# Linear attention and a gated feed-forward layer on one core: queries loaded behind the turned keys, with a new issue order

## The chip, the core and the metric

The kernel runs on one core of a Trainium2 chip. A core has a matrix engine (TensorE, PE in the profile), a vector engine (VectorE, DVE), an activation engine (ScalarE, ACT), a general engine (GpSimd, POOL) and a synchronisation engine (SyncE, SP). Each runs its own instructions in order and waits on semaphores for the others. Transfers between the chip's memory (HBM), the on-chip memory (SBUF) and back run on 16 DMA engines; here GpSimd issues the loads that change float32 into bfloat16, and SP issues the transposes inside SBUF and the stores of the output. TensorE writes its results to eight banks of PSUM, which the other engines read.

The metric is the time of one execution on the device in microseconds (us), the median of several. A profiled execution shows when each instruction ran; its span runs from the program's first instruction to its last.

## What is computed

The inputs are float32: q, k and v of 8 batches, 8 heads, 1024 positions and 64 features; E and F of 64 x 1024; the weights of the layer, 512 x 1536 twice and 1536 x 512.

```python
k_proj = np.einsum('ks,bhsd->bhkd', E, k)
v_proj = np.einsum('ks,bhsd->bhkd', F, v)
scores = (1.0 / np.sqrt(64)) * np.matmul(q, k_proj.transpose(0, 1, 3, 2))
scores = scores - np.max(scores, axis=-1, keepdims=True)
attn = np.exp(scores)
attn = attn / (np.sum(attn, axis=-1, keepdims=True) + 1e-09)
attn_out = np.matmul(attn, v_proj)
x = attn_out.transpose(0, 2, 1, 3).reshape(8 * 1024, 512)
gate = 1.0 / (1.0 + np.exp(-(x @ w_gate)))
out = (gate * (x @ w_val)) @ w_out
```

The 1024 positions of k and v are projected to 64, so that a query meets 64 keys. The output has 8192 rows of 512.

## The kernel before

**Batches and blocks.** The attention goes batch by batch, counted from 0 here; the layer behind it goes in 16 blocks of 512 rows, two a batch. The first batch has code of its own (`first_batch`), with the first block of the layer in plain products. From then on the layer of one batch runs interleaved with the attention of the next, and with the loads of the one after.

**The attention of one batch.** Six loads bring its inputs, each 512 KB as stored in bfloat16: two halves (by heads) of K, of V and of Q (`load_kv`, `load_q`, both through `load`, line 557). K and V go to the two halves of one buffer, `KVs`. Q goes to `Qb`. Then:

- `transpose_q` (line 1438, on SP) turns the queries with four transposing transfers, `Qb` into `qT`.
- `kv` projects K and V, 16 matmuls on TensorE; ScalarE copies the results out, the keys into `kpd`, and `turn_kd` (line 1481, on SP) turns these with one transposing transfer into `kpD`.
- `score_pair` makes the scores of 128 queries in two banks; VectorE takes the maximum (`highest`, line 1590) and subtracts it (`lower`, line 1617); ScalarE writes the exponentials (`exps`) into the K half of `KVs`, which is called `pt` then.
- `turn_p` (line 1652, on SP) turns `pt` into `eT`, four transposing transfers a batch.
- `outs` multiplies with the projected values, VectorE inverts the sums, and VectorE or GpSimd divides (line 1699) into the V half of `KVs`, called `xt` then.
- `turn_x` (line 1716, on SP) turns `xt` into one of two buffers `xT`, four transposing transfers a batch.

So the K and V of the next batch can only be loaded when `pt` and `xt` have been turned. The queries have a buffer of their own, which is free as soon as `transpose_q` has read it.

**The layer.** The gate and value products of a block go in three quads (`quad_jobs`, `seven`): a 2 x 2 matrix of tiles is multiplied with seven products instead of eight, at the price of sums of tiles on VectorE and GpSimd (`xS`, `hT`, line 545, and lines 1102 and 1171) and copies on ScalarE (line 530). Its output product is made in the same way (`o_jobs`) for most blocks. Nearly all matmuls are of 128 x 128 weights and 256 columns, and all stand under line 516.

**The order.** The body is written as jobs, each for one engine. A table, `ORDER`, lists all jobs in the order in which they are issued, which fixes the order on each engine. A negative entry -m is a filler: a matmul of 256 m columns whose result nobody reads, during the start. A second table, `PLACES`, gives each result its PSUM bank or its SBUF buffer. Waits follow from the order: `add` records which tiles a job reads and writes, and each instruction waits for the last writers and readers of them that were issued before it. `ORDER` interleaves the engines, so one can count how many matmuls are issued between, say, a turn and the first matmul that reads it.

**The loads and what they wait for.** `loads` (line 1786) issues the six loads of a batch from 2 on. It is handed `after`, and each of the loads counts these as tiles that it reads:

```python
landed_x = lambda s: [("xTt", s, t, R) for t in range(4) for R in range(2)]
...
loads(2, AT["loads2"], landed_x(1))
...
loads(p + 2, base + AT["loads"], landed_x((p + 1) % 2))
```

So all six loads of a batch wait for the last `turn_x` of the batch in front. GpSimd issues them, and a load that waits holds up what stands behind it on GpSimd: divisions of the attention and sums of the layer. SP's queue is in order too: turns of queries, keys, probabilities and x, and the stores (line 1257).

Of the kernel before, what the change touches and what calls it, by code (L numbers as in the profile page):

```python
# [153 lines left out]
class Job:  # L154
# [189 lines left out]
class Scheduler:  # L344
# [4 lines left out]
    def job(self, eng, pos, body, release=0.0, name=""):  # L349
        self.jobs.append(Job(eng, body, name))  # L350
# [24 lines left out]
def bass_linformer_attn__then__ffn_glu_sigmoid_kernel(  # L375
# [20 lines left out]
    with contextlib.ExitStack() as es:  # L396
# [363 lines left out]
        job = sched.job  # L760
# [1118 lines left out]
```

## Time and profile before

| | us |
|---|---|
| median of three executions | 520.29 |
| lowest, highest | 520.05, 520.41 |
| the profiled execution | 520.55 |
| its span | 518.7 |
| VectorE busy | 434.2 (84%) |
| ScalarE busy | 373.0 (72%) |
| GpSimd busy | 171.5 (33%) |

TensorE's row and the waits are shown where the prediction uses them. TensorE had its full clock throughout. The profile gives DMA queues beside the engines: the loads from GpSimd are in the queue `software_dynamic`, the turns and stores from SP in `hardware_dynamic`. A DMA issue has two times: that of the issuing instruction, and that from its start to the landing of the data. In the order of time, a row holds the start, the time from the first to the end of the last instruction of the row, the engine, the line, the tiles (written, then read), the number of instructions, and in brackets the idle time of that engine in front, with what ended it.

### The profile page before, as it was taken

How to read it: one execution, taken by the hardware profiler on the slowest of the kernel's cores; microseconds unless marked ns; L12 is line 12 of the kernel's file. 1: busy time of each engine (PE TensorE's matmuls, PEld its weight loads, DVE VectorE, ACT ScalarE, POOL GpSimd, SP SyncE). 2: the span in 40 equal slices, each digit the busy share in tenths (PEclk: the TensorE clock that was granted, in tenths of full speed). 3: DMA queues.
4: the chain of work that ended last, by engine and by line, in shares of the span. 5: the costliest groups of instructions: out<-in, count | busy, mean ns of one | idle time of the engine just before them, and what ended most of it. 6: DMA issues, size and time to landing. Idle time of an engine off the chain costs nothing.

```text
span 518.7 us, 12593 instructions
## 1 busy us (share of the span) xinstructions
PE 510.6 (98%) x4954; PEld 418.9 (81%) x4954; DVE 434.2 (84%) x847; ACT 373.0 (72%) x714; POOL 171.5 (33%) x200
## 2 busy tenths in 40 slices
PE   8999999989999999999999999999999999999997
PEld 4557757878888888888888888888888878888884
DVE  6779998498988998889897899899977889958872
ACT  1558776877877787857977778876878669677752
POOL 9885005702226007340157003630243300450020
PEclk9999999999999999999999999999999999999999
DMA  9999949994579955995659935899448983352004
GB/s 165 197 198 207 174 78 174 146 192 124 99 144 168 178 132 95 191 182 137 103 104 206 191 113 90 159 204 158 86 102 165 191 155 83 62 121 84 1 2 162
DMA packets 140556, 71.61 MB, mean 138 GB/s; under 512 B 97232, under 2 KB 132304, under 8 KB 140496
## 3 DMA queue, kind: packets, MB, share of 16 engines
q1 hardware_dynamic: 104560, 40.91, 38.2%
q0 software_dynamic: 35936, 29.89, 37.2%
q8 instruction: 39, 0.64, 0.5%
q14 instruction: 21, 0.17, 0.1%
HBM read 60.29 MB, written 16.78 MB: 149 GB/s over the span
## 4 chain that ended last, share of the span: by engine, by line
PE 92%; DMA 4%; POOL 1%; DVE 1%; ACT 0%; issue 0%; POOLq 0%; ACTq 0%
PE pF L516 50%; PE pA L516 43%; DMA KVs<-in_k_dram 3%; DMA eT<-KVs 1%; POOL hT L545 1%; DVE topf L1590 1%; DMA kpD<-kpd 1%; DVE pF L1617 0%; ACT KVs L530 0%; POOL xS L545 0%; POOL KVs L557 0%; POOL Qb L557 0%; ACT EFT L530 0%; DVE pA L1617 0%; ACT ost L530 0%
## 5 line engine op out<-in xcount | busy, mean ns | idle before, releaser
L530 ACT ACTIVATE spare<-pF 128x512 f32<-128x512 f32 (+2 forms) x163 | 93.2, 580 | 40.0 <-PE pF L516 31.4
L530 ACT ACTIVATE spare<-pA 128x512 f32<-128x512 f32 (+2 forms) x157 | 87.0, 571 | 29.2 <-PE pA L516 18.7
L545 POOL TENSOR_TENSOR hT<-hT,hS 128x512 bf16<-128x512 bf16 x42 | 48.2, 1163 | 160.1 <-PE pF L516 84.2
L1699 POOL TENSOR_TENSOR KVs<-spare,inv 128x384 bf16<-128x384 f32 (+1 forms) x50 | 35.9, 730 | 106.2 <-PE pA L516 31.9
L516 PE MATMUL pF<-wO,hT 128*128 128x256 bf16 (+1 forms) x408 | 60.3, 291 | 0.0
L1171 DVE SCALAR_TENSOR_TENSOR hT<-spare,pA 128x512 bf16<-128x512 f32 x60 | 40.6, 680 | 14.2 <-PE pA L516 5.2
L1102 DVE TENSOR_TENSOR spare<-pA,spare 128x512 f32<-128x512 f32 x62 | 41.8, 682 | 12.1 <-PE pA L516 10.0
L530 ACT ACTIVATE spare<-spare 128x512 f32<-128x512 f32 x77 | 47.8, 628 | 4.8 <-DVE spare L1102 4.7
L516 PEld LDWEIGHTS pF<-wO,hT 128*128 128x128 bf16 x408 | 39.3, 98 | 11.8 <-issue 0.4
L1102 DVE TENSOR_TENSOR spare<-pF,spare 128x512 f32<-128x512 f32 x54 | 36.7, 684 | 10.7 <-PE pF L516 7.3
L1171 DVE SCALAR_TENSOR_TENSOR hT<-spare,pF 128x512 bf16<-128x512 f32 x57 | 38.6, 678 | 4.3 <-PE pF L516 2.7
L516 PE MATMUL pA<-xT,wV 128*128 128x256 bf16 (+1 forms) x208 | 34.4, 287 | 0.0
L516 PE MATMUL pA<-xT,wG 128*128 128x256 bf16 (+1 forms) x212 | 33.8, 283 | 0.0
L516 PE MATMUL pF<-xT,wG 128*128 128x256 bf16 (+1 forms) x196 | 32.6, 288 | 0.4 <-issue 0.4
L516 PE MATMUL pF<-xT,wV 128*128 128x256 bf16 (+1 forms) x200 | 32.4, 283 | 0.0
L516 PE MATMUL pF<-xS,tV 128*128 128x256 bf16 x216 | 32.3, 273 | 0.0
L516 PE MATMUL pA<-xS,tG 128*128 128x256 bf16 x208 | 31.1, 273 | 0.0
L516 PE MATMUL pA<-xS,wV 128*128 128x256 bf16 x200 | 29.7, 273 | 0.0
L516 PE MATMUL pF<-wT,hT 128*128 128x256 bf16 x216 | 28.3, 273 | 0.0
L516 PE MATMUL pA<-wO,hT 128*128 128x256 bf16 (+1 forms) x204 | 27.2, 279 | 0.0
L516 PE MATMUL pF<-wT,hS 128*128 128x256 bf16 x204 | 27.2, 273 | 0.0
L516 PE MATMUL pA<-xS,wG 128*128 128x256 bf16 x184 | 27.1, 272 | 0.0
(184 smaller groups left out, 1258.3 us busy)
## 6 DMA issues: line engine op xcount, KB each, us to landing
out_dram<-ost SPq DMA_DIRECT2D x63, 256.0 KB, 2.4
KVs<-in_v_dram POOLq DMA_DIRECT2D x15, 512.0 KB, 10.6
Qb<-in_q_dram POOLq DMA_DIRECT2D x14, 512.0 KB, 10.2
KVs<-in_k_dram POOLq DMA_DIRECT2D x14, 512.0 KB, 10.7
wO<-in_moe_w_out_dram POOLq DMA_DIRECT2D x1, 1536.0 KB, 12.8
KVs<-in_k_dram POOLq DMA_DIRECT2D x4, 256.0 KB, 6.5
Qb<-in_q_dram POOLq DMA_DIRECT2D x4, 256.0 KB, 9.1
wG<-in_moe_w_gate_dram POOLq DMA_DIRECT2D x4, 256.0 KB, 11.5
```

What stands on the lines that cost most here:

```text
L516: lambda e: e.matmul(o, lhsT, rhs, **kw),
L530: lambda e: e.activation(o, i, func, scale=scale),
L545: fn = lambda e: e.tensor_tensor(o, a, b, op)
L1102: lambda e: e.tensor_tensor(PB(b)[:, :] if stay else BF(s), PB(b)[:, :], BF(s), ALU.add),
L1171: lambda e: e.scalar_tensor_tensor(o, y.rearrange("p (j c) -> p j c", j=2), 1.0, x.rearrange("p (j c) -> p j c", j=2), ALU.add, ALU.mult,),
L1590: lambda e: e.tensor_reduce((top if by_pe(b, t, y) else topf)[:, n : n + 8], PB(bk)[:, :].rearrange("p (n k) -> p n k", n=8), mybir.AxisLi ...
L1699: fn = lambda e: e.tensor_tensor(xto.rearrange("p (g h d) -> p h g d", g=2, h=H)[:, hh[0] : hh[1], :, :], o[:, :, 0:DH].rearrange("p (h g) ...
```

## The change

Each load of queries of batches 2 to 7 now waits for the turned keys of the batch in front (`kpD`, written by `turn_kd`; for batch 2 by the copy that ends the turn of batch 1's keys on TensorE), and no longer for its turned x. It still waits for the turns that read the old queries. `ORDER` and `PLACES` are new throughout; the jobs, their engines and their bodies are otherwise the same. One filler of 512 columns is gone (fillers of 52 x 256 columns before, 50 after).

```diff
 ORDER = (
-    16, -2, -2, -2, 17, 18, 0, 19, -2, -2, -2, -1, 30, 28, 31, 20, 1, 21, -2, -2, -1, 22, 29, 4, 38, 3, 39, -2,
...
+    16, -2, -2, -2, 17, 18, 5, 19, -2, -2, -2, -1, 30, 20, 31, 28, 0, 21, 29, 4, -2, -2, -2, -2, -1, 32, 38, 1,
...
 )
 PLACES = (
-    0, 3, 4, 3, 2, 1, 6, 1, 5, 0, 0, 3, 0, 1, 2, 2, 4, 3, 1, 0, 1, 1, 0, 3, 3, 6, 3, 7, 7, 8, 2, 11, 4, 5, 3, 6,
...
+    0, 2, 6, 2, 3, 1, 4, 1, 5, 0, 2, 1, 1, 0, 3, 2, 6, 3, 2, 0, 0, 2, 0, 1, 0, 2, 6, 7, 7, 9, 0, 8, 5, 1, 3, 6,
...
 )
...
             for R in range(2):
-                job("POOL", pos + AT["gap"] * (4 + R), lambda R=R: load_q(b, R, after), name="loadq")
+                job("POOL", pos + AT["gap"] * (4 + R), lambda R=R: load_q(b, R, [("kpD", x) for x in range(2)]), name="loadq")
```

What the new tables do to the transfers, told by the number of matmuls issued in front of each:

| loads of batch | before: Q halves | before: first and last of K and V | after: Q halves | after: first and last of K and V |
|---|---|---|---|---|
| 1 | 264, 316 | 328, 344 | 275, 335 | 219, 347 |
| 2 | 804, 828 | 796, 876 | 515, 903 | 799, 839 |
| 3 | 1392, 1424 | 1400, 1482 | 1139, 1213 | 1411, 1509 |
| 4 | 2002, 2014 | 1984, 2068 | 1916, 2115 | 2003, 2073 |
| 5 | 2668, 2678 | 2574, 2630 | 2343, 2693 | 2589, 2685 |
| 6 | 3216, 3224 | 3212, 3248 | 2847, 3119 | 3223, 3301 |
| 7 | 3848, 3902 | 3840, 3894 | 3463, 3705 | 3847, 3913 |

The four turns of probabilities of batch 2 stand at 1132, 1168, 1192 and 1258 before, at 1129, 1161, 1204 and 1260 after; those of batch 4 at 2324, 2360, 2415 and 2440 before, at 2323, 2347, 2420 and 2439 after. In batches 2 to 7 some turns of queries now stand on SP between or ahead of the last turns of x of the batch in front, where before all of them stood behind these. The projections of K and V of batches 1 to 7 begin at matmuls 437, 977, 1581, 2177, 2757, 3401 and 4017 before, and at 456, 972, 1588, 2180, 2756, 3396 and 4008 after; for batch 1 that is K alone, V follows at 585 before and 580 after.

354 rows, old and new, of tables (ORDER, PLACES) are left out of this document.

## The prediction

> **What bounds the kernel now.** I read the page first: busy shares, then the chain that ended last.
>
> ```profile
> span 518.7 us, 12593 instructions
> ...
> PE 510.6 (98%) x4954; PEld 418.9 (81%) x4954; DVE 434.2 (84%) x847; ACT 373.0 (72%) x714; POOL 171.5 (33%) x200
> ...
> PE 92%; DMA 4%; POOL 1%; DVE 1%; ACT 0%; issue 0%; POOLq 0%; ACTq 0%
> ```
>
> TensorE is busy for 510.6 of 518.7 us, and the chain lies on it for 92%. Both programs issue the same matmuls except for one idle-time filler. So nearly everything that the change can gain lies in the 8.1 us in which TensorE was idle. The view of waits, for PE alone, says who ended 4.9 us of that:
>
> ```profile
> PE pA L516 <- DMA KVs<-in_k_dram: 1.4, 1, 1.4
> PE pA L516 <- DVE tV L645: 1.1, 1, 1.1
> PE pF L516 <- issue: 0.8, 2, 0.4
> PE pF L516 <- DMA eT<-KVs: 0.5, 1, 0.5
> PE pF L516 <- ACT KVs L530: 0.5, 1, 0.5
> PE pA L516 <- DMA kpD<-kpd: 0.3, 1, 0.3
> PE pF L516 <- ACT EFT L530: 0.3, 1, 0.3
> ```
>
> Four of the eight waits lie in the loop of batches behind a transfer or the attention's own chain (1.4, 0.5, 0.5, 0.3), one of the two "issue" ones too. The others are the start. Where each one stands, and what it really costs, is read from the order of time on PE; ends of matmuls are modelled, so I compare starts. The longest:
>
> ```profile
> 113.06 0.60 PE L516 MATMUL pA<-xS,tG 128*128 128x256 bf16 x4
> 113.50 0.60 PE L516 MATMUL pF<-xS,tV 128*128 128x256 bf16 x4
> 115.52 1.99 PE L516 MATMUL pA<-KVs,EFT 128*64 128x512 bf16 x16 [1.42 <-DMA KVs<-in_k_dram]
> ```
>
> Four matmuls of 256 columns follow each other at 0.44 us, 0.109 us each. The projection of batch 2's keys and values was due at 113.50 + 0.44 = 113.94 and started at 115.52: 1.58 us lost.
>
> **Why it is late.** The chain of waits, and GpSimd's own order of time:
>
> ```profile
> 102.18 13.29 DMA KVs<-in_k_dram
> ```
>
> ```profile
> 93.87 0.81 POOL L557 DMA_DIRECT2D KVs<-in_v_dram  x1 [2.46 <-issue]
> 94.67 0.75 POOL L557 DMA_DIRECT2D Qb<-in_q_dram  x1
> ...
> 97.26 0.79 POOL L557 DMA_DIRECT2D Qb<-in_q_dram  x1
> ...
> 102.18 0.78 POOL L557 DMA_DIRECT2D KVs<-in_k_dram  x1
> ```
>
> All six loads stand behind the last transpose of x; the last half of K goes out as the sixth and takes 13.29 us, because five others, two of them queries, are ahead of it. DMA in the window from 94 to 116 us, then in a quiet one from 126 to 146:
>
> ```profile
> q0 software_dynamic: 3168, 3.15, 89.7%
> ...
> qT<-Qb SPq DMA_TRANSPOSE x4, 10.4
> ```
>
> ```profile
> eT<-KVs SPq DMA_TRANSPOSE x4, 3.1
> xT<-KVs SPq DMA_TRANSPOSE x2, 3.1
> ```
>
> The loads' queue takes 89.7% of 22 us, so one 512 KB load costs 0.897 x 22 / 6 = 3.3 us of it. A transpose beside the loads takes a median of 10.4 us from issue to landing, alone 3.1.
>
> **The change part by part.** *The queries' wait.* In the new order 9 of the 12 query loads of batches 2 to 7 are issued before the K and V loads of their batch; the second of batches 2, 4 and 5 comes behind them. Before batch 2's last K half there are then three loads, not five: it lands 2 x 3.3 = 6.6 us earlier, near 108.9, and was wanted at 113.94. The wait goes whole: **-1.58**. It needs no luck with GpSimd: that load now stands behind two sums on GpSimd, before behind four, and by
>
> ```profile
> DMA to landing us min/median/max: 5.4/11.0/19.7
> ```
>
> the shortest landing of any load from GpSimd is 5.4 us, so even issued at 102.18 with an empty queue it would land at 107.6.
>
> *The other waits.*
>
> ```profile
> 87.51 0.82 PE L516 MATMUL pF<-wT,hT 128*128 128x256 bf16 x6
> 88.78 0.60 PE L516 MATMUL pF<-xT,wG 128*128 128x256 bf16 x4 [0.45 <-issue]
> ```
>
> ```profile
> 232.84 0.60 PE L516 MATMUL pF<-xS,tV 128*128 128x256 bf16 x4
> 233.49 2.01 PE L516 MATMUL pA<-KVs,EFT 128*64 128x512 bf16 x16
> ```
>
> ```profile
> 252.71 0.60 PE L516 MATMUL pF<-xS,tG 128*128 128x256 bf16 x4
> 253.77 0.34 PE L516 MATMUL pF<-vpD,eT 128*128 128x130 bf16 x3 [0.47 <-ACT KVs L530]
> ```
>
> ```profile
> 375.80 0.82 PE L516 MATMUL pF<-wT,hT 128*128 128x256 bf16 x6
> 377.10 0.29 PE L516 MATMUL pF<-vpD,eT 128*128 128x130 bf16 x2 [0.48 <-DMA eT<-KVs]
> ```
>
> ```profile
> 423.51 0.60 PE L516 MATMUL pA<-xS,wG 128*128 128x256 bf16 x4
> 424.46 0.20 PE L516 MATMUL pA<-kpD,qT 64*128 64x64 bf16 x1 [0.35 <-DMA kpD<-kpd]
> ```
>
> By the same reckoning they cost 0.62 (due 88.16), 0.21 (due 233.28), 0.62 (due 253.15), 0.64 (due 376.46) and 0.51 (due 423.95).
>
> The one at 424.46 is a query load's:
>
> ```profile
> 404.89 16.28 SPq L1438 DMA_TRANSPOSE qT<-Qb  x4
> 421.27 1.27 SPq L1481 DMA_TRANSPOSE kpD<-kpd  x1
> ```
>
> SP runs in order: the turn of the keys stood behind four turns of queries whose load came last. In the new order both query loads of that batch go out before its K and V, and the four turns stand ahead of its last two turns of x or right behind. Then kpD waits for the projection alone: **-0.51**. The 0.21 at 233.49 is the projection of batch 4 behind its K; one query load is gone from ahead of it: **-0.21**. At 88.78 the first gate product waits for turned x (both programs turn it from the same work); the new order puts 42 matmuls between the later of the two turns and that product, before 36, which is 6 x 0.109 = 0.65 us more cover: bounds 0 and -0.62, I take **-0.4**. The waits at 253.77 and 377.10 come from the chain scores, maximum, subtraction, exponential, turn, which no load touches. A new order has its own such places. Bounds: both go (-1.26), or three more come, one in every second batch (+1.9); with nothing to choose by, **0**.
>
> *The filler.*
>
> ```profile
> L516 PE MATMUL pA<-ident 128*128 128x512 bf16 x24 | 6.9, 381 | 0.0
> ```
>
> One filler of 512 columns is left out: 2 x 0.109, **-0.2**, or 0 if the data behind it comes no earlier.
>
> *The start.* One V half of batch 1 is now loaded ahead of wO, so K's last half, the fourth load behind wO as before, lands up to one load, 3.3 us, later. Its reader comes 19 matmuls later (about 2 us). Before, neither it nor the scores waited:
>
> ```profile
> 57.55 1.17 PE L516 MATMUL pF<-KVs,EFT 128*64 128x256 bf16 x15
> ```
>
> ```profile
> 68.01 0.20 PE L516 MATMUL pF<-kpD,qT 64*128 64x64 bf16 x1
> ```
>
> Bounds 0 and 3.3 - 2 = 1.3 us; I take **+0.5**, since the queue's work up to there is the same in sum.
>
> *What the early query loads meet.* They now fly while probabilities and x are turned. GpSimd waits at the head of its queue for kpD and for the turns of the old queries; behind the waiting load stand divisions and sums of h, whose readers are turns of x and output products tens of matmuls later, and in every batch kpD is due before that load's place. So the wait itself I cost at nothing; if that cover is gone, a division is late and with it a turn of x. The transfer is the true cost. With one query load in flight instead of six loads, a turn is between 3.1 us (alone) and 10.4. One late turn in the old trace gives the cover:
>
> ```profile
> 372.15 4.90 DMA eT<-KVs
> ```
>
> It landed 1.8 us over 3.1 and cost 0.64, so 1.2 us were covered. The middle price is the page's median for turns of queries, which run beside a varying number of loads:
>
> ```profile
> qT<-Qb SPq DMA_TRANSPOSE x28, 5.8
> ```
>
> 5.8 - 3.1 - 1.2 = 1.5 us a place. In the new order a query load goes out among the turns of probabilities at three places (twice in batch 2's, once in batch 4's). There the order leaves more room than before for the turn hit first: 71 matmuls from turn to first reader, before 55, and 97, before 69. Beside batch 2's second query load it leaves less: 50 for eT2, before 67, and 40 for eT3, before 43. Bounds 0 and 3 x 1.5 = 4.5; I take **+0.5**, nearer to a turn alone: one load holds the engines for 3.3 us of the 20 us window in which six turns went out at 3.1 each.
>
> The Trainium skill, DMA: Bandwidth & Descriptors, section "Issuing engines are not separate DMA queues", speaks against the change here: transfers of whatever engine run on the same 16 DMA engines and interleave. The 10.4 against 3.1 agrees. By it every early query load would stretch each turn that it meets, which is the first rival below.
>
> **Sum.** The profiled execution took 520.55 us, 1.85 outside its span, 0.26 over the median of 520.29. -1.58 - 0.51 - 0.21 - 0.4 + 0 - 0.2 + 0.5 + 0.5 = -1.9: 518.65 by this execution, **518.4** as a median. All bounds at their best: 520.3 - 1.58 - 0.51 - 0.21 - 0.62 - 1.26 - 0.2 = 515.9; all at their worst, 520.3 - 2.3 + 1.9 + 1.3 + 4.5 = 525.7.
>
> **The rivals.** *Early loads delay the turns (slower).* A query load beside the turns of probabilities in batches 2 and 4 holds each by 5.8 - 3.1, past the 1.2 us of cover. From 2.4 us in sum it outweighs the other terms (2.9 - 0.5). At 4.5: 520.3 - 2.9 + 0.5 + 4.5 = 522.4. For it: the 10.4 us. Against: one load in flight, and the longer distances.
>
> *The new order waits elsewhere (no change).* DVE is busy 84% and the old order had only five waits of some 0.6 us in the loop. Three more of these (+1.9) leave 520.3 - 1.9 + 1.9 = 520.3. For it: all issue orders and banks are new. Against: in the loop both orders keep at least eight 256-column matmuls between a bank's filling and the next matmul that needs it read.
>
> *The load is late anyway.* If the three query loads left behind K and V, or GpSimd's sums, held K as before, 1.58 and 0.21 stay: 520.2. The 107.6 above speaks against it; it counts with no change.
>
> **How the numbers follow.** Forecast 0.60, no change 0.17, early loads 0.23. The forecast's own range is 516.5 to 519.2. The range has to leave out no more than 2 in 10: below 516.5 nearly every wait must go, and the slower case counts up to 522.2. 0.2% of 520.3 is 1.04 us, about what a measurement of this kernel can tell from no change: faster 0.60, same 0.17, slower 0.23.
>
> **What would show it.** Right: no wait of PE for KVs, none for kpD, the last K half of batch 2 landing near 109. The early loads are wrong if eT or xT have a median landing well over 3.1 or PE waits for eT more than once. The start is wrong if PE waits before 70 us for K or qT. The whole is wrong if PE's idle sum stays near 8 us, or if the same idle time stands behind DVE and ACT instead of transfers.

## The result, and the profile after

| | before | after |
|---|---|---|
| median, us | 520.09 (20 executions) | 521.25 (20 executions) |
| lowest to highest, us | 519.57 to 521.3 | 519.66 to 523.07 |
| the profiled execution, us | 520.55 | 522.58 |
| its span, us | 518.7 | 520.7 |

The ratio of after to before is 1.002, with a 95% interval of 1.0011 to 1.003. So the change makes the kernel slower by about 1.1 us, where 1.9 us of gain were forecast. Its times also spread over 3.4 us, before over 1.7 us, and the profiled execution is one of the longer ones: 1.3 us over the median.

The page of the changed kernel, its span, the busy shares and the chain that ended last:

```profile
span 520.7 us, 12607 instructions
...
PE 510.6 (98%) x4948; PEld 417.7 (80%) x4953; DVE 435.6 (84%) x847; ACT 373.0 (72%) x714; POOL 173.3 (33%) x200
...
PE 86%; DMA 8%; DVE 2%; POOL 1%; ACT 1%; issue 1%; SPq 0%; POOLq 0%; ACTq 0%; DVEq 0%
```

TensorE is busy for the same 510.6 us, so the 2.0 us of span are idle time. (The 4948 matmuls stand beside 4953 weight loads: five records of matmuls are missing from this trace.) The chain's share on transfers went from 4% to 8%. The view of waits of TensorE says which transfers (what waited, what ended the wait, us in total, times, longest):

```profile
PE pA L516 <- DVE tV L645: 1.1, 1, 1.1
PE pA L516 <- DMA KVs<-in_v_dram: 1.0, 1, 1.0
PE pF L516 <- DVE KVs L1699: 0.7, 1, 0.7
PE pA L516 <- issue: 0.7, 2, 0.5
PE pA L516 <- DMA eT<-KVs: 0.6, 1, 0.6
PE pF L516 <- DMA eT<-KVs: 0.6, 1, 0.6
PE pF L516 <- DMA kpD<-kpd: 0.5, 1, 0.5
```

The wait of 1.4 us for K is gone, as forecast. In its place stand two waits for turned probabilities (`eT`), one for a V half, one for the turned keys, one for a division. TensorE's order of time gives the place of four of them:

```profile
136.43 0.60 PE L516 MATMUL pF<-xT,wV 128*128 128x256 bf16 x4
137.67 0.35 PE L516 MATMUL pA<-vpD,eT 128*128 128x130 bf16 x3 [0.64 <-DMA eT<-KVs]
...
143.63 0.82 PE L516 MATMUL pA<-wO,hT 128*128 128x256 bf16 x6
145.08 0.29 PE L516 MATMUL pF<-vpD,eT 128*128 128x130 bf16 x2 [0.62 <-DMA eT<-KVs]
...
241.48 0.82 PE L516 MATMUL pF<-wT,hT 128*128 128x256 bf16 x6
242.82 0.20 PE L516 MATMUL pF<-kpD,qT 64*128 64x64 bf16 x1 [0.52 <-DMA kpD<-kpd]
...
355.25 0.40 PE L516 MATMUL pA<-KVs,EFT 128*64 128x512 bf16 x1
356.65 1.91 PE L516 MATMUL pA<-KVs,EFT 128*64 128x512 bf16 x15 [1.00 <-DMA KVs<-in_v_dram]
```

From start to start, as in the prediction, they cost 0.80 (137.67 - 136.43 - 0.44), 0.79 (145.08 - 143.63 - 0.66), 0.69 and 1.19 us (the last takes 0.21 for its first matmul). Two of the four waits lie in batch 2's attention. What flew there, from GpSimd's order of time, SP's, and the chain:

```profile
128.06 0.78 POOL L557 DMA_DIRECT2D Qb<-in_q_dram  x1
...
134.50 0.80 POOL L557 DMA_DIRECT2D Qb<-in_q_dram  x1
```

```profile
127.16 1.23 SPq L1652 DMA_TRANSPOSE eT<-KVs  x1
128.43 0.58 SPq L1257 DMA_DIRECT2D out_dram<-ost  x1
130.51 4.36 SPq L1652 DMA_TRANSPOSE eT<-KVs  x2
137.17 1.23 SPq L1716 DMA_TRANSPOSE xT<-KVs  x1
140.05 2.94 SPq L1652 DMA_TRANSPOSE eT<-KVs  x1
```

```profile
130.51 7.11 DMA eT<-KVs
...
140.05 4.98 DMA eT<-KVs
```

Batch 3's two query loads go out at 128.06 and 134.50. The second turn of probabilities, 2.45 us behind the first load, takes 7.11 us to land; the fourth, 5.55 us behind the second load, takes 4.98. A turn alone takes 3.1.

### The profile page after: what moved, and what is told of

Read it like the earlier page. It is cut to its first block, busy times and chain, and to the rows that moved or that the text cites. A ratio compares the mean times of both kernels' runs of the same rounds, so it can differ in the third digit from the quotient of the medians.

```text
span 520.7 us, 12607 instructions
## 1 busy us (share of the span) xinstructions
PE 510.6 (98%) x4948; PEld 417.7 (80%) x4953; DVE 435.6 (84%) x847; ACT 373.0 (72%) x714; POOL 173.3 (33%) x200
## 4 chain that ended last, share of the span: by engine, by line
PE 86%; DMA 8%; DVE 2%; POOL 1%; ACT 1%; issue 1%; SPq 0%; POOLq 0%; ACTq 0%; DVEq 0%
PE pF L516 44%; PE pA L516 43%; DMA eT<-KVs 2%; DMA KVs<-in_v_dram 2%; DMA Qb<-in_q_dram 2%; DMA kpD<-kpd 1%; DMA xT<-KVs 1%; POOL KVs L557 1%; ACT KVs L530 0%; DVE topf L1590 0%; DVE hT L1171 0%; ACT spare L530 0%; POOL KVs L1699 0%; DVE pF L1617 0%; ACT ost L530 0%
## 5 line engine op out<-in xcount | busy, mean ns | idle before, releaser
L1171 DVE SCALAR_TENSOR_TENSOR hT<-spare,pF 128x512 bf16<-128x512 f32 x69 | 46.7, 680 | 12.1 <-ACT spare L530 5.6
L516 PE MATMUL pA<-wO,hT 128*128 128x256 bf16 (+1 forms) x322 | 46.6, 288 | 0.2 <-issue 0.2
L516 PE MATMUL pF<-wO,hT 128*128 128x256 bf16 (+1 forms) x285 | 40.9, 285 | 0.3 <-issue 0.2
L516 PE MATMUL pF<-xT,wV 128*128 128x256 bf16 (+1 forms) x244 | 39.6, 285 | 1.0 <-DVE KVs L1699 0.7
L1171 DVE SCALAR_TENSOR_TENSOR hT<-spare,pA 128x512 bf16<-128x512 f32 x48 | 32.1, 678 | 7.2 <-PE pA L516 6.0
L516 PEld LDWEIGHTS pA<-wO,hT 128*128 128x128 bf16 x324 | 31.2, 98 | 8.3
L516 PEld LDWEIGHTS pF<-wO,hT 128*128 128x128 bf16 x288 | 27.6, 98 | 6.9 <-ACT pF L530 0.4
L557 POOL DMA_DIRECT2D Qb<-in_q_dram x18 | 14.1, 782 | 48.4 <-ACT spare L530 20.0
L516 PE MATMUL pF<-xS,wV 128*128 128x256 bf16 x200 | 30.0, 273 | 0.0
L516 PEld LDWEIGHTS pF<-xT,wV 128*128 128x128 bf16 x244 | 23.1, 98 | 6.7 <-DVE KVs L1699 1.0
```

What stands on the lines that cost most here:

```text
L516: lambda e: e.matmul(o, lhsT, rhs, **kw),
L557: add("POOL", lambda e: e.dma_start(o, i), r=r, w=w, dma=sem, cost=0.78, nbytes=nbytes)
L1171: lambda e: e.scalar_tensor_tensor(o, y.rearrange("p (j c) -> p j c", j=2), 1.0, x.rearrange("p (j c) -> p j c", j=2), ALU.add, ALU.mult,),
```

## The experiments

Two theories stood against each other: the early loads delay the turns, or the new order has waits of its own, whatever the loads do. Each time below stands beside the kernel before on the same chip, whose medians were 519.69 to 520.09. Chips differ by 0.4 us in this, so two edits that ran on different chips are compared by their distances from the kernel before.

| edit | median, us | ratio to before, 95% interval |
|---|---|---|
| the change | 521.25 | 1.002 (1.0011 to 1.003) |
| old order, new wait alone | 523.24 | 1.0057 (1.0042 to 1.0073) |
| old order, queries early | 537.85 | 1.0347 (1.0324 to 1.037) |
| new order, queries late | 548.05 | 1.0526 (1.0504 to 1.0547) |
| new order, old wait | 530.9 | 1.0198 (1.0178 to 1.0218) |
| new order, no wait | 521.6 | 1.0028 (1.0013 to 1.0043) |
| new order, batch 3's loads ahead of the turns | 521.3 | 1.0026 (1.0016 to 1.0036) |
| new order, batch 3's loads late | 519.45 | 0.9999 (0.9989 to 1.0009) |
| new order, second load late | 519.99 | 1.0006 (0.9996 to 1.0016) |
| new order, store sooner | 521.5 | 1.0026 (1.0015 to 1.0036) |
| new order, second load late and store sooner | 519.57 | 0.9993 (0.9983 to 1.0003) |
| new order, two other loads sooner | 521.14 | 1.004 (1.0019 to 1.006) |
| new order, batch 3's late and two sooner | 519.6 | 0.9993 (0.9983 to 1.0003) |
| old order, one early load | 518.37 | 0.9973 (0.9963 to 0.9984) |
| the same, one load among the turns | 518.53 | 0.9974 (0.9963 to 0.9984) |
| the same, that load in the gap | 518.39 | 0.9969 (0.9958 to 0.9979) |
| one load among the turns and a store | 519.69 | 0.9999 (0.9988 to 1.0011) |

**The wait without the order.** The old tables, with only the changed line:

```diff
-                job("POOL", pos + AT["gap"] * (4 + R), lambda R=R: load_q(b, R, after), name="loadq")
+                job("POOL", pos + AT["gap"] * (4 + R), lambda R=R: load_q(b, R, [("kpD", x) for x in range(2)]), name="loadq")
```

> The old order and the old banks, with the new condition of the queries' loads alone. Both theories (early loads delay turns; the new order has waits of its own) expect no change, within 0.3 us of the kernel before: in the old order these loads are issued behind loads of keys and values, or directly in front of one, which still wait for the last turned x, so GpSimd reaches them no sooner. If the condition itself brought the gain that I forecast, it would be 1.6 to 1.9 us faster, with no wait of TensorE for batch 2's keys near 115 us.

Measured: 523.24 us, 3.3 us slower; both theories missed. Each engine's instructions are the same as before. GpSimd's order of time and the chain show the one place (in the chain: start, us, what):

```profile
150.39 0.80 POOL L557 DMA_DIRECT2D Qb<-in_q_dram  x1
```

```profile
150.75 8.10 DMA xT<-KVs
```

```profile
160.63 1.04 PE L516 MATMUL pF<-xS,tG 128*128 128x256 bf16 x4 [2.41 <-ACT pF L530]
161.46 1.06 PE L516 MATMUL pF<-xT,wG 128*128 128x256 bf16 x4
```

In batch 3 a query load stands in front of the K and V loads. It no longer waits for the last turn of x, goes out 0.36 us in front of that turn, and the turn takes 8.10 us; in the old kernel the slower of the same two turns took 4.6. A sum on VectorE is late, then a copy on ScalarE, and TensorE stands for 2.4 us. Behind the wait TensorE is also slower: four matmuls take 0.83 us from start to start (161.46 - 160.63) in place of 0.44, and the granted clock, 1.00 from 150 to 160 us, is 0.59 from 160 to 162. The 16 matmuls from 160.63 on take 3.27 us in place of 1.74, so this adds 1.5 us in this execution. The old condition had held the load back until nothing was left to be turned.

**Early and late loads in both orders.** Two kernels were to complete a square. In the first the old tables have the loads where the change put them (only in batches 6 and 7 the second load stands beside the first). Batch 2's first load and batch 3's two:

```diff
-    ... 436, 453, 456, 420, 469, 523, ... 831, 896, 824, 666, 826, 894, ... 902, 829, 835, 665, 834, 903, ...
+    ... 293, 278, 439, 420, 276, 294, ... 790, 757, 713, 666, 590, 600, ... 759, 755, 801, 665, 614, 707, ...
```

> The old order and banks, with the new condition, and the twelve query loads of batches 2 to 7 moved to where the changed kernel has them; the turns of queries stay where they were. Early loads as the cause: the wait for batch 2's K (1.58 us) and the one for kpD near 424 us (0.51) go, and two or three waits for eT of 0.6 to 0.8 us come in batches 2 and 4, so 0 to 0.8 us faster than the kernel before. The order's own waits as the cause: only the gains are left, 1.8 to 2.3 us faster than the kernel before. If the loads bring nothing at all: no change.

Measured: 537.85 us, not what either theory gave. 7.5 us stand at one place that the edit itself made; the chain:

```profile
67.97 5.46 DMA Qb<-in_q_dram
73.44 0.02 issue
73.46 1.02 ACT kpD L530
```

The load was put ahead of ScalarE's copy into `kpD`. It counts the tile as read, so the copy waits for the load's landing. Collisions are a second part: in batch 2 two turns of probabilities take 7.56 and 7.70 us in the trace, and TensorE loses 3.4 us at one of them. The third part is TensorE's clock, which falls with both waits: 0.50 is granted from 75 to 80 us and 0.86 from 150 to 160, in place of 1.00. The page has TensorE busy for 4.8 us more than before with the same matmuls:

```profile
PE 515.4 (96%) x4949; PEld 419.6 (78%) x4954; DVE 435.3 (81%) x847; ACT 373.7 (70%) x714; POOL 171.5 (32%) x200
```

In the second the new tables have the loads, and their turns, back at the old places. In batches 2 and 4 two turns came to stand ahead of the load that they read, so half of the turned queries are the batch's in front there, and that load waits for these turns at the head of GpSimd's queue. For batch 2 (jobs 420 and 419 are its loads, 421 to 424 its turns):

```diff
-    ... 294, 420, 213, ... 518, 424, 535, ... 525, 419, 546, ... 498, 423, 699, ... 689, 421, 778, 509, 422, 777, ...
+    ... 560, 469, 420, 456, 453, ... 459, 483, 424, 422, 421, 423, 419, 559, ...
```

> The new order and banks, but the twelve query loads of batches 2 to 7 and their turns stand where the old order has them (by the number of matmuls in front). Early loads as the cause: the two waits for eT in batch 2 (0.64 and 0.62 us in brackets), the one for batch 6's V (1.00) and the one for x of batch 4 (0.65) go, the wait for K of batch 2 (1.4 to 1.6) and perhaps one for kpD come back: about 0.5 to 1.5 us faster than the changed kernel, that is within 0.6 us of the kernel before. The order's own waits as the cause: those behind VectorE and ScalarE stay and K's comes on top, 1 us or more slower than the kernel before.

Measured: 548.05 us. Two waits of 7.3 and 9.7 us are that hold, which keeps loads and sums behind it from going out; TensorE's clock falls behind them too (it is busy for 516.4 us). The run says nothing on the theories; the square stayed open and was replaced by smaller edits.

**The conditions in the new order.** The new tables with the old condition, and with none:

```diff
-load_q(b, R, [("kpD", x) for x in range(2)])
+load_q(b, R, after)
```

> The changed kernel's order and banks with the old condition. In this order the condition on turned x falls on an x of three batches earlier wherever a query load stands among the turns of probabilities or ahead, so those loads wait for nothing but the turns of the old queries. If the places in the order are the cause: as slow as the changed kernel, 520.8 to 521.8. If the wait for kpD, with GpSimd held by it, is the cause: the load in batch 2 goes out some us earlier, the waits for eT become shorter, and the time is 0.5 to 1.5 us under 521.3.

```diff
-load_q(b, R, [("kpD", x) for x in range(2)])
+load_q(b, R, [])
```

> The changed kernel's order and banks; the query loads wait for nothing but the turns that read the old queries. If places in the order are the cause and the wait for the turned keys binds nowhere that matters: 520.8 to 521.8, as the changed kernel. If the wait for the turned keys costs by holding GpSimd: 0.5 us or more under 521.3. The slow time with the old condition in this order (530.9) would then come from the turns of x, which there have to wait for the query load that counts their buffer as read; without any condition that hold is gone, so nowhere near 530.

Measured: 530.9 and 521.6 us. Without a condition the time is that of the change: GpSimd issued the load in batch 2 at 128.41, no earlier than with it, because three sums are ahead. The condition on x is another thing. The view of SP's waits there, from 130 to 146 us:

```profile
SPq L129 <- DMA Qb<-in_q_dram: 6.6, 1, 6.6
```

Here the load reads a buffer of x that is about to be written, and SP's next turn of x waits 6.6 us for the load, with a turn of probabilities behind it. TensorE loses 2.15 us there, at 146.69. The same hold comes once more in batch 5, for 8.4 us; the K and V of batch 6 go out late behind it, and TensorE loses 3.0 us at 362.23 (1.19 there in the changed kernel). The granted clock is 0.72 in the 6 us behind each of the two waits. The tile named in a condition also holds its next writer: the old condition could not stay with the new order. Between the new condition and none these runs show no difference.

**Batch 3's loads moved.** First ahead of the turns:

```diff
-    ... 757, 713, 794, 666, 591, 772, ... 755, 801, 606, 665, 730, 802, ...
+    ... 710, 430, 763, 665, 666, 711, 785, ...
```

> The changed kernel, with batch 3's two query loads moved from among the turns of batch 2's probabilities to some 90 matmuls (about 10 us) in front of the first of them. Early loads as the cause: the two waits for eT near 138 and 145 us go and nothing comes for them, 1.0 to 1.6 us faster than the changed kernel, which is 0.0 to 0.5 us faster than the kernel before. The order's own waits as the cause: the two waits are there in some executions only, and the time stays within 0.4 us of the changed kernel, about 1 us over the kernel before.

Then beside K and V, as before the change:

```diff
-    ... 757, 713, 794, 666, 591, 772, ... 755, 801, 606, 665, 730, 802, ...
+    ... 835, 898, 848, 666, 661, 833, ... 903, 849, 662, 665, 852, 914, ...
...
-load_q(b, R, [("kpD", x) for x in range(2)])
+load_q(b, R, after if b == 3 else [("kpD", x) for x in range(2)])
```

> The changed kernel, with batch 3 alone put back: its two query loads stand beside its K and V again and wait for the turned x, and its four turns of queries stand behind the last turns of x. If the early loads among batch 2's turns of probabilities are the cause: the two waits for eT near 138 and 145 us (0.80 and 0.79 us from start to start) go, batch 3's projection of keys starts 1.3 to 1.6 us earlier than in the changed kernel, and the median is 1.0 to 1.6 us under 521.3, that is 519.7 to 520.3. If the new order's own waits are the cause: within 0.4 us of 521.3. If K and V of batch 3 need what the early loads gave them: a wait for KVs near 175 us takes the gain back.

Measured: 521.3 us ahead of the turns, 519.45 us late. Ahead, GpSimd had to wait for the turned keys, and the pair went out from 123.1 us on, still in flight when the first turn started:

```profile
127.80 5.70 DMA eT<-KVs
```

One wait of 1.3 us took the place of two. Late, both waits are gone. Changed kernel and this one issue TensorE's work in the same order, so its starts can be compared; batch 3's projection, changed kernel first:

```profile
176.36 0.84 PE L516 MATMUL pA<-KVs,EFT 128*64 128x512 bf16 x6
```

```profile
174.61 2.23 PE L516 MATMUL pA<-KVs,EFT 128*64 128x512 bf16 x16
```

1.75 us, of which 0.12 was there at batch 2's projection already (114.02 and 113.90). This is the 1.59 of the two waits. The medians say 1.4 us: the change lies 1.16 us over the kernel before on its chip, this one 0.24 under it on its own.

**One load, two loads, a store.** One load at the same place in the old order turned out to cost nothing (below). The traces differed by a store of 256 KB which the new order issues 0.4 us behind the load. Three edits of the changed kernel, all on one chip: the store sooner; batch 3's second load (with its two turns) late; both.

```diff
-    ... 666, 591, 772, 577, 714, 797, ...
+    ... 747, 690, 428, 577, 703, 748, ...
```

> The changed kernel, with one store of the output issued behind the turn of batch 2's keys in place of between the first two turns of its probabilities. If load and store together stretch the turn: the second turn of probabilities lands 4 to 4.6 us after its issue in place of 7.1, the wait near 138 us is gone, the one near 145 us stays, and the median is 0.4 to 0.9 us under 521.3, that is 520.4 to 520.9. If the load alone does it: 7 us, the wait stays, 521.0 to 521.6.

```diff
-    ... 755, 801, 606, 665, 730, 802, ...
+    ... 903, 849, 662, 665, 852, 914, ...
...
-load_q(b, R, [("kpD", x) for x in range(2)])
+load_q(b, R, after if b == 3 and R == 0 else [("kpD", x) for x in range(2)])
```

> The changed kernel, with batch 3's second query load and its two turns put back beside and behind K and V; the first load and the store stay. If each load makes its own wait: the wait near 145 us goes, the one near 138 us stays, 520.3 to 520.9. If the two loads together make both waits: both are gone and 519.4 to 520.0, as with both loads late.

> Both edits: the second load late and the store sooner, so that the first load alone flies among the turns. If one load without a store is covered in the new order as it is in the old: no wait for eT in batch 2 and 519.3 to 520.0, as with both loads late (519.45). If one load costs here whatever flies beside it: a wait of 0.5 us or more and 520.2 or more.

Measured: 521.5, 519.99 and 519.57 us. Batch 2's four turns from issue to landing in the changed kernel, with the store sooner, and with the second load late:

```profile
DMA to landing us min/median/max: 3.1/5.0/7.1
```

```profile
DMA to landing us min/median/max: 3.0/5.1/7.1
```

```profile
DMA to landing us min/median/max: 3.0/4.1/5.6
```

The store is not it: 7.1 us with and without. The second load is: it starts while the second turn still flies. Without it that turn lands after 5.6 us (5.2 with the store sooner as well) and no wait for `eT` is left in batch 2, though the first load flies beside it. With the store sooner in both, the second load alone is worth 1.9 us (521.5 against 519.57).

It does not stretch the same turn each time. Of the five traces that have both loads at these places, the second turn took 7.0 to 7.1 us in four and 5.6 in one (with no condition); that one waited for the fourth turn alone, 0.94 us. In the trace with two other loads sooner it was the other way round: 7.0 us and, for the fourth turn, 3.4, with one wait of 0.69.

How much a turn may take follows from its place. The reader of the second turn was due at 136.87 (136.43 + 0.44), 6.36 us behind the turn's issue: 5.2 to 5.6 us fit, 7.11 don't. The reader of the fourth was due at 144.29 (143.63 + 0.66), 4.24 us behind its issue: 4.98 don't fit. The first load had landed at 135.05, 5 us before the fourth turn went out, so that turn met the second load alone. For the second turn the order's longer distance covers one load, as the prediction had it, and doesn't cover two; for the fourth, which has less distance, one load was enough. No run has the second load without the first.

**The two other waits of the loop.**

```diff
-    ... 1235, 1233, 1412, 1030, 1217, 1223, ... 2018, 1932, 1956, 1755, 1946, 1935, ...
+    ... 1290, 1271, 1025, 1030, 1272, 1230, ... 1899, 1925, 1754, 1755, 2003, 1928, ...
```

> The changed kernel, with batch 4's second query load ahead of one sum on GpSimd and batch 6's last V half ahead of two. If the occasional waits for kpD near 243 us (0.69) and for V near 357 us (1.19) make up the wide spread of the changed kernel (3.4 us from lowest to highest): both are gone, the highest run comes down by 1 us or more, and the median falls by 0.3 to 0.8, to 520.5 to 521.0. If the median's loss lies in batch 2's turns alone: the median stays within 0.3 us of 521.3 and only the highest runs go.

Together with batch 3's loads late:

> The changed kernel with batch 3's queries late (519.45 us before) and, on top, batch 4's second query load ahead of one sum on GpSimd and batch 6's last V half ahead of two. If the wait for kpD near 240 us, which five traces of the new order show at 0.3 to 1.1 us, is what is left: it is gone and the median is 518.6 to 519.2. If the new order loses the rest elsewhere (its start, the gate product near 90 us, the attention's chain): 519.2 to 519.7, and still over the 518.4 of the old order with one early load.

Measured: 521.14 us (520.22 to 522.88 but for one of 527.25) and 519.6 us. The waits for V near 357 us and for `kpD` near 243 us are not in the first trace, but the median is that of the change, and the spread stays; in the second a wait of 0.45 us for `kpD` is back at 241. So these two don't make the median.

**The old order with one early load.** Batch 2's first query load stands behind the copy of batch 1's turned keys, all else is as before:

```diff
-    ... 436, 453, 456, 420, 469, 523, ...
+    ... 276, 294, 320, 420, 217, 547, ...
...
-load_q(b, R, after)
+load_q(b, R, [("kpD", x) for x in range(2)] if b == 2 else after)
```

> The old order and banks; only one query load of batch 2 is moved, to the place behind the turned keys of batch 1, with the new condition for batch 2 alone. Nothing is turned by a transfer there until batch 1's probabilities, 80 matmuls later. If my term for K is right (one load less ahead of K's last half is 3.3 us, and the wait was 1.58): no wait for K near 115 us, and 1.2 to 1.6 us faster than the kernel before, 518.4 to 518.8. If even this load delays the turns of batch 1's probabilities: a wait for eT between 75 and 90 us and no gain. If GpSimd or another load holds K: no change.

Measured: 518.37 us, 1.3 us faster than before (0.9973, interval 0.9963 to 0.9984). TensorE's order of time at batch 2's projection:

```profile
113.11 0.60 PE L516 MATMUL pF<-xS,tV 128*128 128x256 bf16 x4
113.64 1.92 PE L516 MATMUL pA<-KVs,EFT 128*64 128x512 bf16 x16
```

No wait for K. On top of it, batch 3's first load alone, with the new condition for it, among batch 2's turns; then that load in the gap behind the turned keys instead; then the first of these with a store right behind the load:

```diff
-    ... 831, 896, 824, 666, 826, 894, ...
+    ... 790, 757, 713, 666, 590, 600, ...
```

> The old order and banks with the early query load of batch 2 (518.4 us before), and batch 3's first query load alone put where the changed kernel has it: behind the first of the four turns of batch 2's probabilities. The old order leaves 67 matmuls, not 71, from the second turn to its first reader. If one load in flight is what stretches a turn: a turn of probabilities takes 6.5 to 7.5 us from issue to landing in place of some 3.2, one wait for eT of 0.8 to 2.5 us stands in batch 2, and the time is 519.2 to 520.9. If it takes two loads, or the new order itself, to make the wait: 518.4 and no wait.

```diff
-    ... 831, 896, 824, 666, 826, 894, ...
+    ... 761, 690, 428, 666, 748, 749, ...
```

> The same, but that load stands right behind the turn of batch 2's keys, some 120 matmuls in front of the first turn of its probabilities. It can go out when the turned keys have landed, near 121 us; a load takes 5 to 7 us to land with nothing ahead of it, and the first turn of probabilities goes out near 126 to 127. If collisions in time are the cause: the load is nearly through, turns take under 5 us, and the time is 518.2 to 518.9. If an early load costs wherever it stands (GpSimd held at the head of its queue, or DMA work added there): 519.2 or more.

```diff
-    ... 762, 708, 429, 577, 695, 703, ...
+    ... 757, 713, 666, 577, 590, 600, ...
```

> The old order with two early loads (518.53 us before), and one store of the output put between the first two turns of batch 2's probabilities, right behind the load. If load and store together stretch the turn: the second turn of probabilities lands in some 7 us in place of 4.25, a wait for eT of 0.5 to 1.5 us comes, 519.0 to 520.0. If the store matters nothing: 518.2 to 518.8.

Measured: 518.53, 518.39 and 519.69 us. Batch 2's four turns in the three:

```profile
DMA to landing us min/median/max: 3.0/3.1/4.2
```

```profile
DMA to landing us min/median/max: 3.0/3.1/3.2
```

```profile
DMA to landing us min/median/max: 3.0/3.6/5.2
```

One load among the turns stretches one of them by 1.1 us at most and costs nothing that can be told; my expectation of a wait was wrong. In the gap it meets no turn at all. With the store beside it a turn takes 5.2 us, a wait of 1.1 us comes in batch 2, and the time rises by 1.1 us (1.4 under the kernel before on its chip without the store, 0.3 with it). The store had landed, at 130.16, when that turn went out at 130.77; but the load took 7.04 us with it and 6.06 without, and so flew beside the turn for 1 us longer. There the shorter distance of the old order is used up by what the new one still covered.

## Why the prediction was wrong, step by step

**K of batch 2 (-1.58): right.** The wait is gone, the last K half goes out at 99.19, behind three loads, and lands 11.8 us later, at 110.9 (109 was forecast, 113.94 the time it was due). That is 4.5 us earlier than before, not 6.6: 3.0 because it went out sooner, and only 1.5 because it took less time to land. The old order with one early load shows the term by itself: 1.3 us.

**The wait for `kpD` (-0.51): gone at 424, but moved.** In the changed kernel 0.69 stands at 242.82, for the reason that the prediction gave for the old one: batch 4's second query load comes last, its turns stand ahead of `kpD` on SP. In order of time, GpSimd's row first:

```profile
226.69 0.78 POOL L557 DMA_DIRECT2D Qb<-in_q_dram  x1
```

```profile
234.20 3.98 SPq L1438 DMA_TRANSPOSE qT<-Qb  x3
238.27 1.34 SPq L1481 DMA_TRANSPOSE kpD<-kpd  x1
```

That load was in the list of those that stay behind K and V; I had not followed it to SP's queue. In batches 2 and 4 all turns of queries still stand behind the last turn of x; the description of the change is wrong for these two. Of the ten other traces of the new order six have 0.3 to 1.1 us there and four nothing.

**The wait at 233.49 (-0.21): right**, batch 4's projection shows none.

**The gate product (-0.4): wrong in this execution.** The wait at 88.78 is gone, as the longer distance said, and 0.85 stands at 90.72, one value product later:

```profile
89.44 0.60 PE L516 MATMUL pF<-xT,wV 128*128 128x256 bf16 x4
90.72 0.61 PE L516 MATMUL pF<-xT,wV 128*128 128x256 bf16 x4 [0.68 <-DVE KVs L1699]
```

Both products read the same turned x, so x is not what was missing. The second goes to a bank whose last contents a division of VectorE still reads, from 90.11 to 90.67. This comes from the new order and banks, which the term had left out. Three of the ten other traces of the new order don't have it.

**The other waits of the attention's chain (0): right in size, by luck.** The old 1.26 went; 266.40 (0.65), 306.92 (0.48) and 442.27 (0.26) came, 1.39. The first of these is a wait for turned x and not for the chain that the prediction had in mind: batch 4's turn at 261.17 took 5.14 us, with a turn of batch 5's queries 1.3 us behind it and a store 2.7 us behind. Which of the two stretched it, no run took apart.

**The start and the filler (+0.5 and -0.2): about 0.1 in sum.** No wait for batch 1's K or turned queries came in this trace. The projection of batch 1's V starts at 71.12 with 580 matmuls ahead, before at 71.58 with 585; five matmuls are 0.55 us. Traces of the new order differ by 0.6 us there, so more can't be read from it.

**What the early query loads meet (+0.5, bounds 0 to 4.5): the step that failed.** It measured 1.59 in the profiled execution, two waits of 0.8 in batch 2. By the distances of the medians from the kernel before, taking both loads away gave back 1.4 us, the second alone 1.2 (1.9 in the pair on one chip).

The reason for taking 0.5, near the lower bound, was wrong: one load was to hold the engines for 3.3 us of some 20. But two loads fly among batch 2's turns, 6.99 and 8.55 us from issue to landing, the second issued before the first had landed. From 128.06 to 143.04 there was no moment without a load in flight. The step also took the places one at a time. It named the shorter distance of the fourth turn (40 matmuls) without giving it a price of its own, and it did not see that the second turn would still fly when the second load came. Of the three places it counted, batch 4's cost nothing: its turn, 0.33 us behind the load, took 7.10 us, and the 97 matmuls covered that. Batch 2's two cost it all. Three more early loads went out among turns of x and were not counted; no wait of TensorE for these x followed in this trace.

The sign that the prediction named for this came half: the median landing of all turns of probabilities on the page is still 3.1 us, but TensorE waited for `eT` twice. The 5.8 us that I took as the middle price of a turn was fair (7.1 and 5.0); the choice of 0.5 out of 4.5 was not.

**A term that was missing:** V of batch 6, 1.19 in this execution. Its last half goes out at 344.66, behind two sums on GpSimd, and lands after 11.94 us; before, it went out at 337.02. The prediction looked only at the K of batches 2 and 4.

**The sum.** By the profiled executions: -1.58 - 0.51 - 0.21 + 0.23 + 0.13 + 1.59 + 0.69 + 1.19 = +1.5 of the +2.0 us of span. Of the remaining 0.5, 0.3 stand at the end: TensorE's last matmul starts 1.6 us later than before (516.85 and 515.23), the span ends 2.0 later. The rest wasn't told apart. The median has 1.1, since the waits of 0.69 and 1.19 are not in every trace. The first rival had the sign and the place, at a third of its price; the second (waits elsewhere) holds the rest.

What stays open: with batch 3's loads late the new order stands at 519.45, the old order with one early load at 518.37. Some 0.8 us of this difference are there at batch 2's projection: it starts at 113.90 with five matmuls fewer ahead (972, some 0.55 us), the other's at 113.64 with 977. More than half of that is the gate product's wait, 0.85 there and 0.40 here; the rest lies in the start, and no run took it apart. Why the changed kernel's times spread so widely wasn't settled either; the two loads sooner did not narrow it.

## What to carry to other kernels

A wait can look needless and still keep a transfer away from another that is on the path: before it is loosened, list what is in flight from the new time of issue on, all of it together, and compare each transfer on the path with its reader's distance. One load among covered turns may be free where two are not, and a turn with less distance may not cover even one, so move the one that is late and leave the others; here that was worth 1.3 us, and moving all of them cost 1.1. A tile named as a condition also holds its next writer, so its place in the issue order has to be looked at too.

## What was not expected of the hardware

One load of 512 KB, issued 0.36 us ahead of a transposing transfer, stretched it to 8.10 us, one issued 0.33 us ahead another to 7.10, and one issued 3.0 us ahead to 4.2. Two loads gave 5.6 to 7.7 us. Not every long turn had a load beside it: with batch 3's loads late, one of batch 2's four still took 4.5 us, and no run tells why. That transfers of GpSimd and SP share engines is what the Trainium skill, DMA: Bandwidth & Descriptors, says in its section "Issuing engines are not separate DMA queues", and these runs agree; that the price lies so much with the moment of the meeting, and with what else flies, no row of the old trace had shown.

A long wait of TensorE cost more than itself. Over all runs eight of its waits lasted 1.98 us or more. With seven of them its granted clock fell for some microseconds, to 0.50 from 75 to 80 us behind the one of 7.37 us (old order, queries early); with one of 2.27 us (new order, queries late) it did not. With the 1.42 us of the kernel before it stayed full.
